# A hint for a taken branch, given later: in the middle of the small products in front of the branch

## The chip, the cores and the metric

The kernel runs on one core of one Trainium2 chip. The metric is the device time of one execution in microseconds. Times below are counted from the start of the profiled span. A core has five engines that run their own instruction streams: TensorE (PE; its sequencer, which also starts the weight loads, is shown as PEld or PEq), VectorE (DVE), ScalarE (ACT), GpSimd (POOL) and SyncE (SP), which here only issues DMAs and branches.

## The reference, cut to what matters

Three stages stand one behind the other: a local attention, a dense layer, and a layer of eight experts. Only the last one bears on the change:

```
do_compute = x @ w_skip > 0              # tokens that are computed at all
e_idx = argmax(x[do_compute] @ w_gate)   # the expert of each token
for e in range(8):
    rows = tokens of expert e
    h = maximum(x[rows] @ w1[e], 0)
    y[rows] = gate * (h @ w2[e])
out = x + y   (out = x for the tokens left out)
```

There are 1536 tokens of 512 numbers, and w1[e] is 512 x 1024. How many tokens an expert gets is known only at run time.

## The kernel before, in words

Attention and the dense layer take the first 440 us or so. Then a routing step sorts the tokens: each expert has one small tile of 32 tokens and, behind it, `nt[e]` full tiles of 128 tokens, a number that every engine loads into a register (`pre`, L711, a TENSOR_LOAD).

The function `experts()` (from L687 on) goes through the experts in turn, in an order written out by hand, so that each engine runs its instructions as the code lists them.

- **Full tiles.** They stand behind a branch, `tc.If(nt[e] > 0)` at L738. Inside it one tile is computed by `tile_e` (products at L589 and L606, transposes at L600), then `tc.If(nt[e] > 1)` at L746 and so on, up to a loop for a fourth tile and more. In the program the code of the full tiles stands right behind the branch; the branch is *taken* if there is no full tile, and then it jumps over all of that code.
- **Small tiles.** Behind the full tiles of expert e come the first small products of expert e + 1 (`mm1_s`, L659: 16 products in the program, 32 passes in the trace) and the second small products of expert e (`mm2_s`, L677: 32 in the program, 64 passes), a transpose for the next full tile (`tx`, L575), and a transpose of the small tile (`th_s`, L667). Then the next expert's branch follows. They read raw weights from a ring of 20 buffers, which SP fills (`load_e`, L542).
- **Hints.** `hint(e, n)` emits two instructions on TensorE alone: a comparison of `nt[e]` with n into a register, and a BRANCH_PREFETCH_HINT that reads it. With 0 in the register it says that the branch at level n of expert e will be taken; with 1, that it will not be. All instructions of a hint have L1116 in the trace. `hint(e, 0)`, for the outer branch, is given once for each expert; the inner ones are given at the head of each full tile.

Before, `hint(e + 1, 0)` stands right behind expert e's full tiles, ahead of all small products; for expert 0 it stands ahead of the transpose of the first small tiles (`tx_s`, L650).

Of the kernel before, what the change touches and what calls it, by code (L numbers as in the profile page):

```python
# [20 lines left out]
E, F = 8, 1024  # L21
# [40 lines left out]
def body(ctx: ExitStack, tc: tile.TileContext, a):  # L62
# [482 lines left out]
    def wraw(e, k):  # L545
        return raws[(8 * e + k) % NRAW]

    def split_e(e, k, c, sh=5):
        w, r = hl[k], wraw(e, k)
        A.activation(out=w[0][:, c], in_=r[:, c], func=AF.Copy)  # L550
        m = c.start + (c.stop - c.start) * sh // 8
        for eng, d in ((V, slice(c.start, m)), (G, slice(m, c.stop))):
            if d.start < d.stop:
              eng.tensor_tensor(out=w[1][:, d], in0=r[:, d], in1=w[0][:, d].bitcast(F32), op=ALU.subtract)  # L554
# [3 lines left out]
    def gather(xg, ix):  # L558
        nc.gpsimd.indirect_dma_start(out=xg, out_offset=None, in_=xs[:, :],
                                     in_offset=IndirectOffsetOnAxis(ap=ix, axis=0))  # L560

    def scatter(ix, xg):
        nc.gpsimd.indirect_dma_start(out=a["out"], out_offset=IndirectOffsetOnAxis(ap=ix, axis=0),  # L563
                                     in_=xg, in_offset=None, bounds_check=NT - 1, oob_is_err=False)
# [7 lines left out]
    def tx(xg, i):  # L572
        ps = psa.tile([128, 4, 128], F32, tag="a", name="pstx")
        for k in range(4):
            T.transpose(ps[:, k, :], xg[:, k * 128:(k + 1) * 128], ident)  # L575
        split_t((sl["x"][:, i, 0:4], sl["x"][:, i, 4:8]), ps)
# [66 lines left out]
    def ga_s(g):  # L643
        xsm[g] = gp.tile([128, DM], F32, tag="xg", name="xsm", bufs=2)
        gather(xsm[g], col(idx, E, g))

    def tx_s(g):
        ps = psa.tile([128, 4, 128], F32, tag="a", name="pstxs")
        for k in range(4):
            T.transpose(ps[:, k, :], xsm[g][:, k * 128:(k + 1) * 128], ident)  # L650
        for i in range(2):
            A.activation(out=xq[g][i], in_=ps[:, 2 * i:2 * i + 2], func=AF.Copy)

    def mm1_s(e):
        ps = psh.tile([128, 256], F32, tag="h", name="ps1")
        o = SM * (e % 4)
        for k in range(4):
            for j in range(4):
                T.matmul(out=ps[32 * j:32 * j + 32], lhsT=xq[e // 4][k // 2][:, k % 2, o:o + SM],  # L659
                         rhs=wraw(e, k)[:, 256 * j:256 * j + 256], start=(k == 0), stop=(k == 3))  # L660
        hsm[e] = sl["hr"]
        A.activation(out=hsm[e], in_=ps, func=AF.Relu)

    def th_s(e):
        ps = psa.tile([128, 2, 128], F32, tag="a", name="psths")
        for c in range(2):
            T.transpose(ps[:, c, :], hsm[e][:, c * 128:(c + 1) * 128], ident)  # L667
        hsm[e] = sl["hq"]
        A.activation(out=hsm[e], in_=ps, func=AF.Copy)

    def mm2_s(e):
        po = pso.tile([128, 128], F32, tag="o", name="pos")
        for f in range(8):
            w = wraw(e, 4 + f // 2)
            for j in range(4):
                o = 512 * (f % 2) + 128 * j
                T.matmul(out=po[32 * j:32 * j + 32], lhsT=hsm[e][:, f % 2, 32 * (f // 2):32 * (f // 2) + 32],  # L677
                         rhs=w[:, o:o + 128], start=(f == 0), stop=(f == 7))
        o, g = SM * (e % 4), e // 4
        for j in range(4):  # L680
            x = xsm[g][o:o + SM, 128 * j:128 * j + 128]
            V.scalar_tensor_tensor(out=x, in0=po[32 * j:32 * j + 32], scalar=col(gat, E, g)[o:o + SM], in1=x,  # L682
                                   op0=ALU.mult, op1=ALU.add)
        if e in SC:
            o = SC[e]
            n = SM * (e % 4 + 1)
            scatter(sl["ix"] if o else col(idx, E, g)[0:n], xsm[g][o:n])  # L687

    def col(t, e, j):
        return t[:, e * NJ + j:e * NJ + j + 1]  # L690

    def experts():
        sl["x"] = xts.tile([128, 2, 8, 128], F32R, tag="xt", name="slx")
        sl["h"] = xts.tile([128, 2, 8, 128], F32R, tag="xt", name="slh")
        sl["hr"] = ep.tile([128, 256], F32, tag="u", name="hr")
        sl["hq"] = ep.tile([128, 2, 128], F32, tag="n", name="hq")
        for g, tags in enumerate((("hn", "hn"), ("u", "n"))):
            xq[g] = [ep.tile([128, 2, 128], F32, tag=t, name=f"xq{g}{t}") for t in tags]
        xf = []
        for _ in range(2):  # L700
            t = stg.tile([128, 2, DM], F32, tag="stg", name="xh")
            xf.extend([t[:, 0], t[:, 1]])
        xf.extend(x2p.tile([128, DM], F32, tag="x2", name=f"xf{i}", bufs=3) for i in (4, 5))
        nt = {}

        def ga_f(e):
            if e < E:
                gather(xf[e % 3], col(idx, e, 1))

        def pre(e):  # L710
            nt[e] = nc.values_load(nti[0:1, e:e + 1], min_val=0, max_val=NJ - 1)  # L711

        def hint(e, n):
            tc.mark_branch_hint_location(f"t{n}{e}", hint=(nt[e] > n), engines=[mybir.EngineType.PE])

        def presplit(e):
            for k in range(4):
                split_e(e, k, C0, SH)

        sl["ix"] = rp.tile([SM, 1], I32, tag="r2", name="ix7")  # L720
        ga_s(0)
        ga_f(0)
        ga_f(1)
        ga_s(1)
        pre(0)
        hint(0, 0)
        presplit(0)
        tx_s(0)
        mm1_s(0)
        st["gates"]()  # L730
        tx(xf[0], 0)
        for e in range(E):
            fa, fb, fc, fd = xf[e % 3], xf[3], xf[4], xf[5]
            if e + 1 < E:
                pre(e + 1)
            if e < E - 1:
                th_s(e)
            with tc.If(nt[e] > 0, label=f"t0{e}"):  # L738
                hint(e, 1)
                gather(fb, col(idx, e, 2))  # L740
                tile_e(0, fa, col(idx, e, 1), col(gat, e, 1),
                       {0: [lambda k=k: split_e(e, k, C1, SI) for k in range(4)],
                        1: [lambda: split_e(e, 4, CA)], 2: [lambda: split_e(e, 5, CA)],
                        3: [lambda: split_e(e, 6, CA)], 4: [lambda: split_e(e, 7, CA)],
                        5: [lambda: tx(fb, 1)]})
                with tc.If(nt[e] > 1, label=f"t1{e}"):  # L746
                    hint(e, 2)
                    gather(fc, col(idx, e, 3))
                    tile_e(1, fb, col(idx, e, 2), col(gat, e, 2), {5: [lambda: tx(fc, 0)]})
                    with tc.If(nt[e] > 2, label=f"t2{e}"):  # L750
                        hint(e, 3)
                        tile_e(0, fc, col(idx, e, 3), col(gat, e, 3))
                        with tc.If(nt[e] > 3, label=f"t3{e}"):
                            with tc.For_i(3, nt[e], 1) as j:
                                ixd = rp.tile([128, 1], I32, tag="r1", name="ixd")
                                V.tensor_copy(ixd, idx[:, bass.ds(j + e * NJ + 1, 1)])
                                gtd = rp.tile([128, 1], F32, tag="r4", name="gtd")
                                V.tensor_copy(gtd, gat[:, bass.ds(j + e * NJ + 1, 1)])
                                gather(fd, ixd)
                                tx(fd, 1)  # L760
                                tile_e(1, fd, ixd, gtd)
            load_e(8 * e + 4 + NRAW)
            ga_f(e + 2)
            if e + 1 < E:
                hint(e + 1, 0)
                presplit(e + 1)
                mm1_s(e + 1)
            if e == 2:
                tx_s(1)
            if e < E - 1:  # L770
                mm2_s(e)
            if e == E - 2:
                V.tensor_copy(sl["ix"], col(idx, E, 1)[128 - SM:128])  # L773
                th_s(E - 1)
            if e + 1 < E:
                tx(xf[(e + 1) % 3], 0)
            if e == E - 2:
                mm2_s(E - 1)
            load_e(8 * e + 8 + NRAW)

    two = const.tile([128, 1], F32, name="two")
# [118 lines left out]
    half = {}  # L900
# [156 lines left out]
    with tc.manual_schedule():  # L1057
        experts()
# [61 lines left out]
```

## Time and profile before

| what | value |
| --- | --- |
| median of 3 runs | 605.8 us (605.23 to 607.18) |
| profiled execution | 607.17 us, its span 605.3 us |
| TensorE (PE) busy | 529.5 us, 87% of the span |
| VectorE, GpSimd, ScalarE busy | 451.4, 325.1, 293.5 us |
| first hint on TensorE | at 448.6 us |
| instruction queue q8 | 39 packets, 0.64 MB |

The span is cut into stages with different limits, so the shares say little; the last 157 us, from the first hint on, are those of the experts. The queues named "instruction" bring program code to the engines; they are listed with the other DMA queues. A row with PEldq or PEq is an instruction of TensorE's sequencer that does no arithmetic, such as a branch.

### The profile page before, as it was taken

What the parts mean: (1) busy time and instruction counts of PE and PEld (TensorE: products, weight loads), DVE (VectorE), ACT (ScalarE), POOL (GpSimd) and SP (SyncE); (2) the same over time, 40 slices, a digit from 0 to 9 for tenths busy, and PEclk for the clock granted to TensorE, in tenths of its full rate; (3) what the DMA queues carried; (4) which work ended last, traced back from release to release, by engine and by line L of the source; (5) the groups of instructions that cost most, each with busy time, mean ns of one, the idle gap of its engine ahead of it and who ended that gap; (6) DMA issues with size and microseconds to landing.
All of it is one profiled execution on the core that took longest, in us unless ns stands there. A gap on an engine that the chain in (4) does not pass through costs nothing. (4 is left out here: it accounts for less than half of the span.)

```text
span 605.3 us, 11155 instructions
## 1 busy us (share of the span) xinstructions
PE 529.5 (87%) x3870; PEld 429.3 (71%) x3870; DVE 451.4 (75%) x892; ACT 293.5 (48%) x614; POOL 325.1 (54%) x346
## 2 busy tenths in 40 slices
PE   6679768578887999999999999999879979698994
PEld 3557547457766888898988888988547857476873
DVE  3488999999999866659689697697677357466324
ACT  2746544446454646545444436444526346366321
POOL 5135767766667756435444445445547456667303
PEclk9889798899997999999999999999999999799998
DMA  8919543545421102224100037560137659991100
GB/s 272 322 42 316 158 162 129 173 152 142 125 64 32 47 21 76 86 70 157 34 15 15 1 139 247 206 208 2 58 107 272 228 178 390 324 370 48 35 18 15
DMA packets 40614, 82.57 MB, mean 136 GB/s; under 512 B 4749, under 2 KB 17297, under 8 KB 40536
## 3 DMA queue, kind: packets, MB, share of 16 engines
q1 hardware_dynamic: 38280, 75.03, 36.7%
q0 software_dynamic: 2256, 6.57, 3.4%
q8 instruction: 39, 0.64, 0.4%
q14 instruction: 39, 0.32, 0.2%
HBM read 72.92 MB, written 9.44 MB: 136 GB/s over the span
## 5 line engine op out<-in xcount | busy, mean ns | idle before, releaser
L373 PE MATMUL o<-w,g 128*128 128x512 f32 x576 | 158.0, 411 | 18.9 <-ACT g L343 17.2
L298 PE MATMUL h<-xt,w 128*128 128x384 f32 x768 | 158.6, 350 | 10.4 <-DVE hn L330 5.0
L298 PEld LDWEIGHTS h<-xt,w 128*128 128x128 f32 x768 | 137.5, 194 | 20.0 <-DVE hn L330 8.1
L373 PEld LDWEIGHTS o<-w,g 128*128 128x128 f32 x576 | 105.9, 192 | 44.9 <-ACT g L343 22.7
L331 POOL TENSOR_TENSOR hn<-hn,u 128x384 f32<-128x384 f32 (+1 forms) x66 | 81.1, 1229 | 67.3 <-ACT u L320 30.8
L344 POOL TENSOR_TENSOR g<-hn,g 128x384 fp32r<-128x384 f32 (+1 forms) x66 | 72.3, 1095 | 61.9 <-ACT g L343 61.8
L319 ACT ACTIVATE u<-nn,two 128x384 f32<-128x384 f32 (+1 forms) x66 | 40.0, 606 | 61.0 <-DVE nn L318 60.8
L187 POOL TENSOR_TENSOR w<-r,w 128x512 fp32r<-128x512 f32 x32 | 46.8, 1466 | 42.4 <-ACT w L186 42.4
L554 POOL TENSOR_TENSOR hl<-rawe,hl 128x128 fp32r<-128x128 f32 (+1 forms) x64 | 56.1, 904 | 14.6 <-ACT hl L550 14.0
L343 ACT ACTIVATE g<-hn 128x384 fp32r<-128x384 f32 (+1 forms) x66 | 33.8, 513 | 55.1 <-DVE hn L339 54.3
L339 DVE SCALAR_TENSOR_TENSOR hn<-nn,hn 128x384 f32<-128x384 f32 (+1 forms) x66 | 46.8, 709 | 15.3 <-POOL hn L331 15.1
L318 DVE SCALAR_TENSOR_TENSOR nn<-u 128x384 f32<-128x384 f32 (+1 forms) x66 | 48.0, 728 | 12.5 <-ACT u L312 12.4
L335 DVE SCALAR_TENSOR_TENSOR nn<-nn,u 128x384 f32<-128x384 f32 (+1 forms) x66 | 46.2, 699 | 13.8 <-ACT u L320 13.7
L554 DVE TENSOR_TENSOR hl<-rawe,hl 128x384 fp32r<-128x384 f32 (+1 forms) x64 | 43.6, 719 | 16.4 <-ACT hl L550 14.7
L550 ACT ACTIVATE hl<-rawe 128x512 fp32r<-128x512 f32 (+1 forms) x64 | 43.2, 731 | 11.9 <-PEq L738 4.3
L312 ACT ACTIVATE u<-u 128x384 f32<-128x384 f32 (+1 forms) x66 | 34.0, 515 | 30.8 <-DVE u L311 30.0
L589 PE MATMUL p<-hl,slx 128*128 128x512 f32 x168 | 41.8, 397 | 2.1 <-ACT slx L567 1.6
L606 PE MATMUL po<-hl,slh 128*128 128x512 f32 x168 | 43.1, 399 | 0.0
L311 DVE TENSOR_SCALAR u<-h 128x384 f32<-128x384 f32 (+1 forms) x66 | 35.5, 537 | 4.6 <-PE h L298 4.6
L589 PEld LDWEIGHTS p<-hl,slx 128*128 128x128 f32 x168 | 30.7, 188 | 9.1 <-ACT slx L567 2.3
L606 PEld LDWEIGHTS po<-hl,slh 128*128 128x128 f32 x168 | 30.6, 188 | 6.2
L320 ACT ACTIVATE u<-u 128x384 f32<-128x384 f32 (+1 forms) x66 | 33.6, 510 | 1.1
(175 smaller groups left out, 793.3 us busy)
## 6 DMA issues: line engine op xcount, KB each, us to landing
rawe<-w SPq DMA_DIRECT2D x64, 512.0 KB, 5.8
rawr<-wio SPq DMA_DIRECT2D x30, 512.0 KB, 3.8
vw<-vx SPq DMA_DIRECT2D x40, 97.5 KB, 2.9
xs<-x SPq DMA_DIRECT2D x12, 256.0 KB, 3.9
out<-x SPq DMA_DIRECT2D x12, 256.0 KB, 2.1
kw<-kx SPq DMA_DIRECT2D x18, 160.0 KB, 5.0
q<-qx SPq DMA_DIRECT2D x20, 128.0 KB, 3.4
kt<-kt SPq DMA_DIRECT2D x4, 384.0 KB, 4.2
```

Source lines behind the costliest of these rows:

```text
L187: G.tensor_tensor(out=w[1][:, o:o + 512], in0=r, in1=w[0][:, o:o + 512].bitcast(F32), op=ALU.subtract)
L298: T.matmul(out=h, lhsT=w[wi][:, k * 128:(k + 1) * 128], rhs=x[:, xi, k, :], start=(c == 0), stop=(c == 11))
L318: V.scalar_tensor_tensor(out=nn[:, c], in0=u[:, c], scalar=2.0, in1=u[:, c], op0=ALU.add, op1=ALU.mult)
L331: G.tensor_tensor(out=hn[:, c], in0=hn[:, c], in1=u[:, c], op=ALU.mult)
L335: V.scalar_tensor_tensor(out=nn[:, c], in0=nn[:, c], scalar=2.0, in1=u[:, c], op0=ALU.add, op1=ALU.mult)
L339: V.scalar_tensor_tensor(out=hn[:, c], in0=nn[:, c], scalar=2.0, in1=hn[:, c], op0=ALU.subtract, op1=ALU.mult)
L344: G.tensor_tensor(out=g[:, 1, c], in0=hn[:, c], in1=g[:, 0, c].bitcast(F32), op=ALU.subtract)
L373: T.matmul(out=o_t[t], lhsT=g[:, gi, t * 128:(t + 1) * 128], rhs=w[wi][:, 512:1024], start=(first and i == 0), stop=(end and i == 2))
L550: A.activation(out=w[0][:, c], in_=r[:, c], func=AF.Copy)
L554: eng.tensor_tensor(out=w[1][:, d], in0=r[:, d], in1=w[0][:, d].bitcast(F32), op=ALU.subtract)
L589: T.matmul(out=ps, lhsT=x[:, xi + k, :], rhs=w[wi][:, 512 * half:512 * half + 512], start=(k == 0 and xi == 0 and wi == 0), stop=(k == 3 a ...
L606: T.matmul(out=ps, lhsT=hs[f // 4][:, xi + f % 4, :], rhs=w[wi][:, 512 * (f % 2):512 * (f % 2) + 512], start=(f == 0 and i == 0), stop=(f ...
```

## The change

The hint for an outer branch is given later. For expert 0 it moves behind `mm1_s(0)`. For every other expert it moves into the middle of the last group of `mm2_s` ahead of its branch: `mm2_s` gets an argument, a function that it calls after 4 of its 8 steps. For experts 1 to 6 that group is `mm2_s(e)` of the expert before; for expert 7, whose branch has two such groups in front of it, it is `mm2_s(7)`, the later one.

```
-    def mm2_s(e):
+    def mm2_s(e, half=None):
         po = pso.tile([128, 128], F32, tag="o", name="pos")
         for f in range(8):
+            if f == 4 and half:
+                half()
             w = wraw(e, 4 + f // 2)
...
-        hint(0, 0)
         presplit(0)
         tx_s(0)
         mm1_s(0)
+        hint(0, 0)
...
             if e + 1 < E:
-                hint(e + 1, 0)
                 presplit(e + 1)
                 mm1_s(e + 1)
...
             if e < E - 1:
-                mm2_s(e)
+                mm2_s(e, None if e == E - 2 else lambda: hint(e + 1, 0))
...
             if e == E - 2:
-                mm2_s(E - 1)
+                mm2_s(E - 1, lambda: hint(E - 1, 0))
```

On TensorE's stream, ahead of expert 0's branch, it stood so before (pstxs: the small tiles' transpose, ps: `mm1_s`, psi: gates, pstx: `tx`, psths: `th_s`; lines of the kernel before):

```order
L714 REGISTER_ALU
L1116 BRANCH_PREFETCH_HINT
L650 MATMUL pstxs<-cb,xsm 128x128 x4
L659 MATMUL ps_4890<-rawe_3951,xq0hn 32x256 x4
L659 MATMUL ps_4890<-rawe_3953,xq0hn 32x256 x4
L659 MATMUL ps_4890<-rawe_3955,xq0hn 32x256 x4
L659 MATMUL ps_4890<-rawe_3957,xq0hn 32x256 x4
L495 MATMUL psi<-so 128x104 x6
L575 MATMUL pstx<-cb,xh 128x128 x4
L711 TENSOR_LOAD nti
L667 MATMUL psths<-cb,hr 128x128 x2
L738 COMPARE_AND_BRANCH
```

and so it stands now:

```order
L650 MATMUL pstxs<-cb,xsm 128x128 x4
L659 MATMUL ps_4887<-rawe_3951,xq0hn 32x256 x4
L659 MATMUL ps_4887<-rawe_3953,xq0hn 32x256 x4
L659 MATMUL ps_4887<-rawe_3955,xq0hn 32x256 x4
L659 MATMUL ps_4887<-rawe_3957,xq0hn 32x256 x4
L716 REGISTER_ALU
L1117 BRANCH_PREFETCH_HINT
L495 MATMUL psi<-so 128x104 x6
L575 MATMUL pstx<-cb,xh 128x128 x4
L713 TENSOR_LOAD nti
L667 MATMUL psths<-cb,hr 128x128 x2
L740 COMPARE_AND_BRANCH
```

The hint and its comparison have moved behind the five rows of transposes and `mm1_s`; 12 products, a register load and the waits in between are left ahead of the branch.

Ahead of expert 2's branch TensorE's stream was (pos: `mm2_s` of expert 1):

```order
L1116 BRANCH_PREFETCH_HINT
L659 MATMUL ps_5805<-rawe_4321,xq0hn 32x256 x4
L659 MATMUL ps_5805<-rawe_4323,xq0hn 32x256 x4
L659 MATMUL ps_5805<-rawe_4368,xq0hn 32x256 x4
L659 MATMUL ps_5805<-rawe_4370,xq0hn 32x256 x4
L677 MATMUL pos<-rawe_4199,hq 32x128 x8
L677 MATMUL pos<-rawe_4201,hq 32x128 x8
L677 MATMUL pos<-rawe_4250,hq 32x128 x8
L677 MATMUL pos<-rawe_4252,hq 32x128 x8
L575 MATMUL pstx<-cb,xh 128x128 x4
L711 TENSOR_LOAD nti
L667 MATMUL psths<-cb,hr 128x128 x2
```

and is now:

```order
L659 MATMUL ps_5802<-rawe_4323,xq0hn 32x256 x4
L659 MATMUL ps_5802<-rawe_4368,xq0hn 32x256 x4
L659 MATMUL ps_5802<-rawe_4370,xq0hn 32x256 x4
L679 MATMUL pos<-rawe_4199,hq 32x128 x8
L679 MATMUL pos<-rawe_4201,hq 32x128 x8
L716 REGISTER_ALU
L1117 BRANCH_PREFETCH_HINT
L679 MATMUL pos<-rawe_4250,hq 32x128 x8
L679 MATMUL pos<-rawe_4252,hq 32x128 x8
L575 MATMUL pstx<-cb,xh 128x128 x4
L713 TENSOR_LOAD nti
L667 MATMUL psths<-cb,hr 128x128 x2
```

The hint has moved behind all of `mm1_s` and half of `mm2_s`. The other engines' streams and the number of TensorE's instructions are as before.

## Rows read from the trace of the kernel before

**Rows 1.** The page's first line.

```profile
span 605.3 us, 11155 instructions
```

**Rows 2.** Line 738, TensorE's queue, experts 0, 2, 4, 7: ns min/median/max, start.

```profile
L738 PEldq COMPARE_BRANCH  x1: 1124/1124/1124, 455.0 to 455.0; - x1
...
L738 PEldq COMPARE_BRANCH  x1: 1494/1494/1494, 491.8 to 491.8; - x1
...
L738 PEldq COMPARE_BRANCH  x1: 5687/5687/5687, 518.9 to 518.9; - x1
...
L738 PEldq COMPARE_BRANCH  x1: 2792/2792/2792, 597.3 to 597.3; - x1
```

**Rows 3.** Line 1116, TensorE's hints ahead of the first three.

```profile
L1116 PEldq BRANCH_PREFETCH_HINT  x1: 44/44/44, 448.6 to 448.6; - x1
...
L1116 PEldq BRANCH_PREFETCH_HINT  x1: 39/39/39, 487.4 to 487.4; - x1
...
L1116 PEldq BRANCH_PREFETCH_HINT  x1: 35/35/35, 514.5 to 514.5; - x1
```

**Rows 4.** Windows: length; busy PE, PEld, DVE, ACT, POOL; clock, DMA share, GB/s.

```profile
197.80:419.10 221.30, 219.63 (x1397) 192.46 (x1394) 173.64 (x402) 109.79 (x219) 112.05 (x97) 1.00 0.28 90
455.00:457.00 2.00, 1.21 (x15) 0.89 (x18) 1.40 (x4) 0.96 (x3) 1.06 (x1) 1.00 0.05 14
...
459.00:460.00 1.00, 1.00 (x45) 1.00 (x39) 1.00 (x2) 0.37 (x2) 1.00 (x3) 1.00 0.89 184
...
487.40:490.00 2.60, 2.40 (x57) 1.96 (x61) 2.19 (x5) 2.17 (x5) 1.42 (x2) 1.00 0.18 65
...
518.90:522.10 3.20, 0.77 (x6) 0.53 (x6) 2.10 (x5) 0.87 (x2) 1.78 (x3) 1.00 0.94 262
```

**Rows 5.** Queue q8, windows 197.8:419.1, 453.5:454.8, 456.7:457.8, 490.9:491.9, 513.1:517.5.

```profile
q8 instruction: 11, 0.18, 0.4%
...
q8 instruction: 1, 0.02, 5.1%
...
q8 instruction: 1, 0.02, 5.4%
...
q8 instruction: 1, 0.02, 6.1%
...
q8 instruction: 1, 0.02, 1.6%
```

**Rows 6.** TensorE's timeline ahead of expert 3 and behind expert 4's branch.

```profile
499.54 0.42 PE L677 MATMUL pos<-rawe,hq 128*32 128x128 f32 x6 [1.37 <-issue]
...
525.05 1.94 PE L659 MATMUL ps<-rawe,xq1u 128*32 128x256 f32 x16 [5.38 <-PEq L738]
```

**Rows 7.** TensorE's timeline around expert 0's branch: start, us, group, idle before.

```profile
452.53 1.93 PE L659 MATMUL ps<-rawe,xq0hn 128*32 128x256 f32 x32 [0.53 <-ACT xq0hn L652]
454.39 0.87 PE L495 MATMUL psi<-so 128*128 128x104 f32 x6
...
456.75 1.93 PE L659 MATMUL ps<-rawe,xq0hn 128*32 128x256 f32 x32 [0.79 <-ACTq L738]
458.50 2.04 PE L677 MATMUL pos<-rawe,hq 128*32 128x128 f32 x64
...
461.86 4.40 PE L589 MATMUL p<-hl,slx 128*128 128x512 f32 x18 [0.52 <-issue]
```

**Rows 8.** Waits from 446 to 470 us: who waited for whom, us, times.

```profile
SPq L542 <- DVEq L738: 7.9, 1, 7.9
```

**Rows 9.** TensorE near 188 us; windows of TensorE: length, busy, clock, DMA share, GB/s.

```profile
187.77 2.10 PE L373 MATMUL o<-w,g 128*128 128x512 f32 x6 [2.98 <-ACT g L343]
...
188.80:195.60 6.80, 6.22 (x21) 0.50 0.00 1
...
525.00:530.10 5.10, 5.05 (x64) 0.50 1.03 396
```

**Rows 10.** The chain that ended last: start, us, what.

```profile
596.75 3.09 DMA out<-xsm,idx
```

More of the change, by code (lines that the diff above doesn't have):

```diff
@@ L669, in th_s, with mm2_s @@
         A.activation(out=hsm[e], in_=ps, func=AF.Copy)
-    def mm2_s(e):
+    def mm2_s(e, half=None):
         po = pso.tile([128, 128], F32, tag="o", name="pos")
         for f in range(8):
+            if f == 4 and half:
+                half()
             w = wraw(e, 4 + f // 2)
@@ L725, in experts @@
         pre(0)
-        hint(0, 0)
         presplit(0)
@@ L729, in experts @@
         mm1_s(0)
+        hint(0, 0)
         st["gates"]()
@@ L764, in experts @@
             if e + 1 < E:
-                hint(e + 1, 0)
                 presplit(e + 1)
@@ L770, in experts @@
             if e < E - 1:
-                mm2_s(e)
+                mm2_s(e, None if e == E - 2 else lambda: hint(e + 1, 0))
             if e == E - 2:
@@ L777, in experts @@
             if e == E - 2:
-                mm2_s(E - 1)
+                mm2_s(E - 1, lambda: hint(E - 1, 0))
             load_e(8 * e + 8 + NRAW)
```

## The prediction

> **What bounds the kernel now.** I read the page first and then, for the last quarter of the span, the timeline of TensorE, because that is where the hints stand. There the kernel is one chain on TensorE: eight experts in turn, each with small products on raw weights (L659, L677) and, if the expert has full tiles, the large products (L589, L606) behind a branch at L738. All the rows are from one execution of 607.17 us, whose span is 605.3 us [rows 1]; the median of three runs is 605.8 us. I work with differences and add them to the median.
>
> The branch of an expert without a full tile is taken. That is so for experts 0, 2, 4 and 7, and TensorE's sequencer sat in these four branches for 1.12, 1.49, 5.69 and 2.79 us [rows 2]. A branch that is not taken is quick, and I see nothing to win there. So the question is what sets these four numbers. The hints of the first three stand at 448.6, 487.4 and 514.5 us [rows 3], which is 6.4, 4.4 and 4.4 us ahead of their branches. The lead alone does not explain the wait: two equal leads have 1.5 and 5.7 us behind them.
>
> What explains it is the instruction queue. In a straight run of 221 us it brought 11 packets, 0.18 MB in all, while TensorE started 1397 products and 1394 weight loads [rows 4, 5]; that is one packet of 16 KB for each 254 or so instructions. Counting the built program in steps of 256 from a place where TensorE ran dry (1.37 us without a releaser, six passes before the end of an L677 group [rows 6]) gives the block edges:
> - One edge lies in the warming products just ahead of the first hint. No packet comes from there to 453.5, then one [rows 5]; the branch at 455.0 ends at 456.1. That packet was the branch's target.
> - Expert 2's hint at 487.4 has no packet behind it for 3.5 us, though the DMA was far from busy (0.18 [rows 4]). The packet comes at 490.9 [rows 5], as the sequencer passes an edge inside L677, and the branch ends at 493.3.
> - Expert 4's hint has no edge between it and its branch. The one packet of 513.1 to 517.5 [rows 5] belongs to the code behind the landing of expert 3. The target comes only once the branch asks: 5.69 us.
>
> [...] A hint decides what the next packet is, but the packet is asked for only when an edge is passed (or just has been); with no edge to come, the branch has to ask for itself.
>
> [...]
>
> **The change part by part.** Nothing is added or removed: a register operation and a hint (28 to 44 ns of queue time [rows 3]) move within each group, and the blocks keep their places.
>
> *Expert 0.* The hint moves behind the products of L659, which TensorE runs from 452.53 to 454.4 [rows 7]; the sequencer is somewhat ahead, so I put the hint at 453.3. The edge was passed before 448. [...] So the branch asks for itself. What that costs: the DMA is almost idle there, with a share of 0.05 from 455 to 457 [rows 4]. At its landing at 456.1 the sequencer's next packet followed within 0.7 us, after 456.7 [rows 5]; a packet takes about 1.0 us (5.1% of 16 engines over 1.3 us is 1.06 us [rows 5]), and the branch of expert 2 ended 1.4 us after its packet did. 0.7 + 1.0 + 1.4 = 3.1 us instead of 1.1: **+2.0 us**. Bounds: if the hint is served at once, 453.3 + 3.1 = 456.4, so +0.3; if the branch is as slow as expert 4's, 5.7 - 1.1 = +4.6. I take the idle value, since expert 4's branch stood in a DMA share of 0.94 [rows 4].
>
> *The block behind that landing.* From the landing to the next edge there are about 130 instructions: all of L659 and half of L677. Before, TensorE passed that edge near 459.2, 3.1 us after landing, without a wait, since the packet was asked for at 456.7 in an idle DMA. Now it is asked for at 458.1, after the weight loads of SP have begun (they wait for VectorE's branch [rows 8]) and the share is 0.89 [rows 4]. The nearest row for a landing in a busy DMA is expert 2's: landing at 493.3, TensorE goes on at 499.54 [rows 2, 6], 6.2 us. So 458.1 + 6.2 = 464.3 against 458.1 + 3.1 = 461.2: **+3.1 us**. Bounds: 0 if the packet still comes in time; 3.6 if it is asked for later still. I take 3.1, the only such row.
>
> [...]
>
> *The clock.* TensorE would stand from 456.0 to 458.7. [...] After expert 4's stall, 16 passes of L659 took 1.94 us, where 32 took 1.93 [rows 6, 7]: the lower of the two levels. If it falls here, most of the slow stretch lies where TensorE waits for the block anyway. **+0.6 us**, between 0 and 3.4 (half of 6.8).
>
> *Expert 2.* The new hint still stands some 29 instructions ahead of the edge inside L677, so the same packet is asked for at the same edge: **0**. Bounds: -1.4 if the branch needs no wait at all, +4.2 if it has to ask (5.7 - 1.5).
>
> *Expert 4.* No edge before, none now; the branch asks for itself either way: **0**. Bounds: nothing to lose; the most to win is the 5.6 us of the wait plus half of the 5 us at half speed behind it.
>
> *Expert 7.* Its branch is behind TensorE's last product. The chain ends in the scatter and its landing from 596.75 to 599.84 [rows 10], not in this branch; an edge lies between hint and branch both before and after: **0**, with some 4 us of room before the end of the span at 605.3.
>
> *Experts 1, 3, 5, 6.* Their hints say that the branch is not taken. They leave the place just behind a landing. **0**; bounds -1.4 (the wait at 499.54, if the hint delays that packet) and +3.6 (a packet dropped because expert 1's new hint stands right behind an edge).
>
> What passes through: ScalarE's and GpSimd's splits for expert 1 do not wait for the landing, and L589 at 461.86 already waits for TensorE's own chain alone [rows 7]; from there TensorE is busy without a gap. So the delay is carried to the end. Sum: 2.0 + 3.1 + 0.6 = 5.7 us, 612.9 us on the profiled execution, **611.5 us** on the median.
>
> **The rivals.**
> [...]
> - *A hint has a fixed delay.* If a hint asks at once but takes the time seen with experts 0 and 2 (7.5 and 5.9 us to the end of the branch), a shorter lead costs everywhere: +4.6 at expert 0 (capped by the branch's own asking), +2.3 at expert 2 (hint 2.3 us later), +3.1 for the block: 615.8 us. Against it: the packet of expert 2 came at an edge.
> - *Still in time.* The hint is served at once and quickly: 605.8 + 0.3 = 606.1 us. [...]
> - *Faster: expert 4's hint was lost and no longer is.* At 514.5 the packet behind the landing was still outstanding; a hint given then may be dropped. The new one comes near 516.9, once that packet (of 513.1 to 517.5) is under way. If it then is served with 3.1 us, the branch ends at 520.0 instead of 524.6: -4.6, and the half speed from 525.0 to 530.1 goes [rows 9], -2.5. It decides if it beats the +5.7 of expert 0: 605.8 + 5.7 - 7.1 = 604.4 us, and 602.9 with half of the block term. [...]
>
> **How the numbers follow.** Forecast 0.56, with its own range 608.0 to 615.5; only the branch pays 0.11; fixed delay 0.08; still in time 0.12; faster 0.13. About 0.3%, 1.8 us, is what a measurement of this kernel can tell from no change. Slower by more: 0.54 of the forecast, 0.07 of the second, all of the third: 0.69. Within: 0.02 + 0.04 + 0.12 = 0.18. Faster: 0.13. Leaving out about half of the faster case below, and half of the fixed delay with the forecast's upper tail above, the range is 604.0 to 616.5.
>
> **What would show it.** In the profile of the changed kernel the taken branch of expert 0 lasts about 3.1 us instead of 1.12, with a packet after 455.5; a gap without a releaser of 2 to 3 us stands inside the first L677 group; L589 of expert 1 starts near 467 instead of 461.9; expert 2's branch stays at 1.5, expert 4's at 5.7. I am wrong if expert 0's branch stays under 1.5 us (the hint is served without an edge), or if expert 4's falls below 3 us (the earlier hint was lost).

## The result, and the profile after

The changed kernel is slower: 612.73 us in the median of 7 runs (610.38 to 614.82) beside 607.18 us of the kernel before in the same session (7 runs, 605.23 to 612.1). The ratio is 1.0073 with a 95% interval of 1.0044 to 1.0103, so +4.4 us, between 2.7 and 6.3; the two medians lie 5.6 us apart. The forecast, 611.5 on 605.8, is a ratio of 1.0094: inside the interval.

The profiled execution took 610.38 us; its page begins so, beside [rows 1]:

```profile
span 608.6 us, 11155 instructions
```

The spans differ by only 3.3 us, because in this execution the first branch comes 2.2 us earlier than before. Of that lead 1.5 us are there 25 us into the span and 2.1 by 50 us, long before the first hint. Kernels whose streams are the same up to this branch differ as much (454.97 before, 453.86 and 452.32 in else_3 and else_all below), so I compare from the first branch on: 150.3 us from there to the end of the span before, 155.8 after, +5.5.

The four taken branches (TensorE's queue, line 740 now; ns, start) and the first three hints answer to [rows 2, 3]:

```profile
L740 PEldq COMPARE_BRANCH  x1: 3393/3393/3393, 452.8 to 452.8; - x1
...
L740 PEldq COMPARE_BRANCH  x1: 1623/1623/1623, 493.5 to 493.5; - x1
...
L740 PEldq COMPARE_BRANCH  x1: 6602/6602/6602, 520.3 to 520.3; - x1
...
L740 PEldq COMPARE_BRANCH  x1: 3465/3465/3465, 599.8 to 599.8; - x1
...
L1117 PEldq BRANCH_PREFETCH_HINT  x1: 44/44/44, 450.7 to 450.7; - x1
...
L1117 PEldq BRANCH_PREFETCH_HINT  x1: 35/35/35, 491.2 to 491.2; - x1
...
L1117 PEldq BRANCH_PREFETCH_HINT  x1: 35/35/35, 518.0 to 518.0; - x1
```

Expert 0's branch went from 1.12 to 3.39 us, with the hint 2.1 us ahead of it instead of 6.3. Expert 2's stayed. Expert 4's and expert 7's rose by 0.9 and 0.7 us.

The instruction queue in the windows 450.6 to 452.5, 452.6 to 454.6 and 458.6 to 459.8 us (packets, MB, share of 16 engines), beside [rows 5]:

```profile
q8 instruction: 1, 0.02, 3.3%
...
q8 instruction: 1, 0.02, 2.7%
...
q8 instruction: 1, 0.02, 5.0%
```

The first packet starts at 451.40, 0.75 us behind the hint, and does not serve the branch. The second starts at 453.70, 0.95 us behind the branch's start, and lasts 0.88; the branch ends 1.56 us later. The third is the block behind the landing.

TensorE's timeline there (start, us, group, idle before) answers to [rows 7]:

```profile
450.06 1.93 PE L659 MATMUL ps<-rawe,xq0hn 128*32 128x256 f32 x32 [0.53 <-issue]
...
453.11 0.38 PE L667 MATMUL psths<-cb,hr 128*128 128x128 f32 x2
456.46 3.49 PE L659 MATMUL ps<-rawe,xq0hn 128*32 128x256 f32 x32 [2.96 <-PEq L740]
459.76 1.06 PE L679 MATMUL pos<-rawe,hq 128*32 128x128 f32 x31
461.08 1.29 PE L679 MATMUL pos<-rawe,hq 128*32 128x128 f32 x33 [0.26 <-issue]
...
463.70 1.66 PE L589 MATMUL p<-hl,slx 128*128 128x512 f32 x6 [0.52 <-ACT slx L567]
```

And two windows of it (length, busy PE, clock, DMA share, GB/s), beside [rows 4, 9]:

```profile
456.30:459.70 3.40, 3.24 (x32) 0.50 0.94 278
...
455.00:457.00 2.00, 0.54 (x8) 0.81 0.82 147
```

The reader is to see three things between the branch and L589 of expert 1, which took 6.9 us before and 10.9 now. TensorE stands 2.96 us for the branch. Then the same 32 passes of L659 take 3.49 us instead of 1.93, at a granted clock of 0.50. And the block behind the landing costs one gap of 0.26 us. Worked out: 2.27 (3393 - 1124 ns) + 1.56 + 0.26 = 4.1 us, the difference of the two stretches. The other 1.4 us of the 5.5 are +0.9 in expert 4's branch, +0.9 in the last landing and -0.4 in between. The landing, beside [rows 10]:

```profile
599.16 3.97 DMA out<-xsm,idx
```

### The profile page after: what moved, and what is told of

It reads as the page before. It is cut to its first block, busy times and chain, and to the rows that moved or that the text cites. A ratio compares the mean times of both kernels' runs of the same rounds, so it can differ in the third digit from the quotient of the medians.

```text
span 608.6 us, 11155 instructions
## 1 busy us (share of the span) xinstructions
PE 528.9 (87%) x3870; PEld 428.0 (70%) x3870; DVE 450.5 (74%) x892; ACT 293.2 (48%) x614; POOL 324.8 (53%) x346
## 5 line engine op out<-in xcount | busy, mean ns | idle before, releaser
L373 PEld LDWEIGHTS o<-w,g 128*128 128x128 f32 x576 | 106.1, 193 | 44.9 <-ACT g L343 22.5
L589 PE MATMUL p<-hl,slx 128*128 128x512 f32 x168 | 41.7, 397 | 2.1 <-ACT slx L567 1.6
L589 PEld LDWEIGHTS p<-hl,slx 128*128 128x128 f32 x168 | 30.7, 188 | 9.0 <-ACT slx L567 2.3
```

The source lines that it names most:

```text
L373: T.matmul(out=o_t[t], lhsT=g[:, gi, t * 128:(t + 1) * 128], rhs=w[wi][:, 512:1024], start=(first and i == 0), stop=(end and i == 2))
L589: T.matmul(out=ps, lhsT=x[:, xi + k, :], rhs=w[wi][:, 512 * half:512 * half + 512], start=(k == 0 and xi == 0 and wi == 0), stop=(k == 3 a ...
```

## The experiments

Each time stands beside that of the kernel before from the same session; "to the end" is from expert 0's branch to the end of the span of the profiled execution (before: 150.3 us). With single runs I read only the profile, since runs of the kernel before spread from 604 to 612 us (one of 2789 us is left out).

**Which hint costs the time?** Three kernels, all made from the kernel before.

```
first_only:  -        hint(0, 0)            # ahead of tx_s(0)
             +        hint(0, 0)            # behind mm1_s(0); all other hints as before
rest_only:   the change without its first part: hint(0, 0) stays ahead of tx_s(0)
no_first:    -        hint(0, 0)            # nothing in its place
```

> Only expert 0's hint is given late (behind its L659 products); the other hints stand as before. Theory (a hint sets the next packet, which is asked for at a block edge; expert 0's late hint has no edge left): all of the loss is here. The branch of expert 0 lasts 3.1 to 3.6 us instead of 1.12, L659 behind it runs slowly if the clock falls; 605.8 + 4 = about 1.006 to 1.008 of before. Rival (a hint needs a fixed time, so that every shorter lead costs): about half of the loss, 1.003 to 1.004, since expert 2 and 4 keep their leads.

> Expert 0's hint as before, all others late (middle of L677). Theory: no change, 0.998 to 1.002; branch of expert 0 at 1.1, of expert 2 at 1.5 +- 0.3, of expert 4 at 5.7 or a little more. Rival (fixed time): expert 2's branch rises to 3.5 us or more, 1.004. Rival (expert 4's early hint was lost): its branch falls below 3 us, 0.99.

> Expert 0 gets no hint at all, the others as before. Theory: the late hint of expert 0 did nothing, so this is the same as the late hint: branch 3.1 to 3.6 us, 1.006 to 1.008 of before. Rival (the late hint did start the fetch, about 2 us ahead of the branch): without it the branch lasts 5 to 5.7 us and the time is 1.009 or more.

Measured: first_only 613.76 against 607.59 us, ratio 1.0082 [1.0048, 1.0116]; rest_only 608.31, 1.0009 [0.9977, 1.0041]; no_first 612.90, 1.0079 [1.0054, 1.0104]. Expert 0's branch in first_only and in no_first:

```profile
L738 PEldq COMPARE_BRANCH  x1: 3427/3427/3427, 455.4 to 455.4; - x1
```

```profile
L737 PEldq COMPARE_BRANCH  x1: 3365/3365/3365, 454.8 to 454.8; - x1
```

So, within these intervals, the whole loss is the first hint's, and where the change puts it, the hint is worth nothing that can be measured: without any hint the branch and the time are the same. In both kernels, as in the changed one, the packet starts 0.95 to 0.97 us behind the branch's start.

rest_only also moved expert 4's branch, from 5.7 to 3.3 us, and gained nothing:

```profile
L740 PEldq COMPARE_BRANCH  x1: 3268/3268/3268, 517.1 to 517.1; - x1
```

I come back to that with the last group.

**A block edge, or the lead?** My prediction let a hint work only if TensorE passes a block edge behind it, that is, goes over from one block of the program to the next (a block is what one packet of q8 brings: 254 products and weight loads in the straight run of [rows 4, 5], some 256 instructions with the 32 of TensorE's semaphores among them). Five kernels vary the edge and the lead (the time from a hint to its branch) apart.

```
edge_early: STEPS: z14 -> z34     # 20 more warming pairs at the start; the edge lies 37 instructions earlier
mid_hint:   hint(0, 0) between tx_s(0) and mm1_s(0): 3.5 us ahead of the branch
half_hint:  hint(0, 0) in the middle of mm1_s(0): 2.5 us ahead
edge_late:  the changed kernel, z14 -> z92: the edge lies between the late hint and its branch
mid_early:  edge_early and mid_hint together
```

> Hints as before, but 20 more warming pairs (40 instructions) run on TensorE near the start, so that every block edge falls some 37 instructions earlier in the later code: expert 0's early hint now stands 52 instructions behind an edge and none follows ahead of the branch. The lead of 6.4 us stays. Theory: the branch of expert 0 lasts 3.1 to 3.6 us as with the late hint; expert 2's edge comes 1 us earlier, so its branch falls to 0.4 to 0.8; the dry spell ahead of expert 3 grows from 1.4 to about 2.4 us. Rival (fixed time): branch of expert 0 stays at 1.1, of expert 2 at 1.5.

> Expert 0's hint stands between the transposes (L650) and the products of L659, so about 3.6 us ahead of its branch instead of 6.3 (early) or 2.1 (late); the rest as before. Reading 1 (the packet follows a hint by about 4.9 us, whatever else runs): the packet is not there in time, the branch asks for itself and lasts 3.4 us. Reading 2 (the packet was only held up by the four gathers that run from 447.5 to 452.5): it comes about 1.4 us ahead of the branch as with the early hint, and the branch lasts 1.1 us. Reading 3 (first theory, no edge left after the hint): 3.4 us.

> The kernel before with expert 0's hint alone moved, into the middle of the 16 products of L659 ahead of the branch: a lead of 2.6 to 2.9 us, between the 2.1 us that was worth nothing and the 3.5 us that was enough. If the hint works at once and a packet takes 1 us and its unpacking 1.5: the branch ends 2.5 us behind the hint, so it takes about 1.1 us at most, 151 to 152 us from there to the end. If a hint needs over 3 us, the branch takes 3.4 us as without a hint, 155 to 157 us to the end. A value between (1.5 to 3 us) would say that the branch waits for the rest of a fetch that the hint had begun.

> The changed kernel with 78 more warming pairs (products and their weight loads) at the start, where TensorE waits anyway, so that a block edge lies some 12 instructions behind expert 0's late hint and 16 ahead of its branch. First theory (a packet is asked for only at an edge): the target comes 1 us behind the edge, about at the branch, and the branch of expert 0 takes 1.0 to 1.6 us; the time from that branch to the end is about 151 us. Rival (a lead of 2.1 us is too short wherever the edge lies): the branch takes 3.3 to 3.5 us, 155 to 157 us to the end. If the plain next block is fetched at that edge first and holds the queue, the branch takes over 3.5 us.

> Two edits that each left expert 0's branch at 1.1 us, together: 20 more warming pairs at the start, so that the plain next block is in 5 us before the hint and no packet is outstanding when it comes, and expert 0's hint behind the transpose of the small tiles (a lead of 3.5 us). First theory (a hint turns a packet that is asked for and has not begun into the target; when none is outstanding it asks by itself, but later than 3.5 us): no packet of the queue ahead of the branch, one 1.0 us behind its start, the branch 3.3 to 3.9 us, 154 to 157 us from its start to the end. Rival (a lead of 3.5 us is enough as such; the packet only waits until the gathers are through the DMA): a packet 1.1 us behind GpSimd's last gather ahead of the branch and 1.4 us ahead of the branch, which takes 1.1 us, 150 to 152 us to the end.

Measured for all kernels, by the trace, one execution each (the packet is the one that the branch waited for; its start is counted from the branch's start):

| kernel | lead of the hint, us | packet, us | branch, ns | to the end, us |
| --- | --- | --- | --- | --- |
| before | 6.3 | -1.4 | 1124 | 150.3 |
| edge_early | 6.3 | -1.5 | 1116 | 149.5 |
| mid_early | 3.75 | -1.65 | 880 | 149.3 |
| mid_hint | 3.5 | -1.4 | 1097 | 152.3 |
| half_hint | 2.5 | +0.96 | 3897 | 155.4 |
| after | 2.1 | +0.95 | 3393 | 155.8 |
| edge_late | 2.1 | +1.5 | 3834 | 160.4 |
| no_first | none | +0.96 | 3365 | 155.8 |

The times of the single runs were 606.55 (edge_early), 609.70 (mid_hint), 610.31 (half_hint), 629.81 (edge_late: the 78 pairs hold up the start by some 13 to 15 us and disturb more than the edge: from expert 2's branch to expert 3's it takes 13.8 us, 8.1 in the changed kernel) and 607.20 (mid_early). mid_hint's 152.3 us come from later places: its branches of experts 2, 4 and 7 took 1.0, 0.7 and 1.0 us more than before. My miss shows best in edge_early. Branch and hint, and then the queues in the windows 442.7 to 444.2, 444.2 to 453.6 and 453.6 to 455.0:

```profile
L738 PEldq COMPARE_BRANCH  x1: 1116/1116/1116, 455.2 to 455.2; - x1
...
L1116 PEldq BRANCH_PREFETCH_HINT  x1: 44/44/44, 448.9 to 448.9; - x1
```

```profile
q8 instruction: 1, 0.02, 5.4%
...
q0 software_dynamic: 232, 0.78, 27.5%
q14 instruction: 2, 0.02, 0.8%
...
q0 software_dynamic: 74, 0.24, 50.9%
q8 instruction: 1, 0.02, 4.5%
```

The plain next block was in by 444.1, 4.7 us ahead of the hint, and no edge followed. By my reading nothing should have come, and the branch should have taken 3.4 us. The target came all the same, ahead of the branch. Of the rest of that expectation one half held: expert 2's branch fell to 449 ns, but the dry spell ahead of expert 3, which was to grow, is gone. The reverse is edge_late: hint at 465.5, branch at 467.6, the edge (as the program is laid out) between them. Its queues from 445.4 to 469.0 and from 469.0 to 470.0:

```profile
L740 PEldq COMPARE_BRANCH  x1: 3834/3834/3834, 467.6 to 467.6; - x1
...
L1117 PEldq BRANCH_PREFETCH_HINT  x1: 35/35/35, 465.5 to 465.5; - x1
```

```profile
q0 software_dynamic: 560, 1.84, 22.9%
q1 hardware_dynamic: 432, 0.79, 9.2%
q14 instruction: 2, 0.02, 0.3%
...
q8 instruction: 1, 0.02, 5.7%
```

In the long window there is no row of q8 at all: neither edge nor hint brought a packet in time. So at expert 0 an edge behind the hint is not what it takes: hints 3.5 us and more ahead of the branch worked without one, and hints 2.1 us ahead did not work, with an edge or without, nor did one 2.5 us ahead.

Between the two I tried a last escape, that a hint can only turn a packet that is still outstanding, and asks too slowly by itself. mid_early refutes it; its branch and hint, and its queues from 444.8 to 454.3 and from 454.3 to 455.5:

```profile
L738 PEldq COMPARE_BRANCH  x1: 880/880/880, 456.1 to 456.1; - x1
...
L1116 PEldq BRANCH_PREFETCH_HINT  x1: 40/40/40, 452.3 to 452.3; - x1
```

```profile
q0 software_dynamic: 233, 0.78, 25.9%
q14 instruction: 2, 0.02, 0.7%
...
q0 software_dynamic: 58, 0.19, 54.8%
q8 instruction: 1, 0.02, 5.1%
```

Nothing was outstanding when the hint came, and its packet started 2.1 us later.

That the short lead itself is the cause is not shown. half_hint's branch and hint, and q8 from 449.8 to 451.2:

```profile
L739 PEldq COMPARE_BRANCH  x1: 3897/3897/3897, 453.0 to 453.0; - x1
...
L1117 PEldq BRANCH_PREFETCH_HINT  x1: 44/44/44, 450.4 to 450.4; - x1
...
q8 instruction: 1, 0.02, 4.7%
```

That packet, the plain next block's, ran from 449.91 to 450.97, across the hint. In the changed kernel and in first_only it started 0.75 and 0.5 us behind the hint; in edge_early, mid_hint and mid_early no such packet is near. So a late hint and a plain packet beside it mostly come together, and a rival stands: such a packet holds the hint's own back. Only edge_late has the short lead alone (the packet before its hint started at 444.4), and it is one disturbed execution. else_3 below bears on this too: its stream up to expert 0 is that of the kernel before and its hint stands 6.3 us ahead, but a plain packet came first, 2.1 us behind the hint, the target's 3.4 us after that one, and the branch took 1634 ns. No kernel was made that tells the lead from the packet.

**What holds the packet back?** In the kernel before it came 4.9 us behind the hint, in mid_hint and mid_early 2.1 us. Two kernels change what lies between.

```
late_gathers: ga_f(1), ga_s(1) moved from ahead of hint(0, 0) to behind presplit(0)
fill_behind:  FW = (4, 4, 4, 16) -> (4, 4, 4, 4), and behind hint(0, 0) the same 12 warming products
```

> Hints as before, but the third and fourth gather on GpSimd (experts 1's tile and the second group of small tiles) are issued behind the splits of expert 0, so that less DMA runs between expert 0's hint and its branch. Reading 1 (fixed 4.9 us): packet 4.9 us behind the hint, branch 1.1 us. Reading 2 (held up by the gathers): packet 2 to 3.5 us behind the hint, branch under 0.3 us, and TensorE goes on about 0.9 us earlier against the branch's start.

> Hints as before, but 12 of the 16 warming products in front of expert 0's register load run behind its hint, so that the hint stands 9 instructions ahead of a block edge instead of 15 behind it; the hint still cannot run before the register is loaded (at 448). First theory (the packet is asked for at an edge): packet about 1 us behind the hint, the branch of expert 0 under 0.3 us, 0.998 of before. Reading 1 or 2 (4.9 us, or the gathers): packet 4 to 5 us behind the hint, branch 1.1 us, 1.000.

late_gathers: one run of 611.09 us against 608.57; the packet starts 3.8 us behind the hint and 2.6 us ahead of the branch, which takes 479 ns. fill_behind: 607.33 against 608.57, ratio 0.9993 [0.9969, 1.0017]; the packet starts 5.3 us behind the hint and 2.35 us ahead of the branch, 479 ns again. With half of the gathers moved back by some 1.6 us the packet came 1.1 us sooner behind the hint. In the kernel before, edge_early, mid_hint and mid_early it starts 0.8 to 1.1 us behind the end of GpSimd's fourth gather, in fill_behind 1.5. Both fit a packet that waits behind the gathers in the DMA; they do not prove it, since in late_gathers it comes 2.6 us behind the end of the second gather and while the third is being issued. What is shown is that the branch of the kernel before could still be 0.65 us shorter, and that this alone is too little to be seen in the time.

**Expert 4's branch.** Its stall of 5.7 us was the prize of my "faster" rival. Two kernels give its hint earlier, in the arm that runs when expert 3 has no further tile.

```
else_3:    with c1.Else(): hint(e + 1, 0)     # for e == 3 alone, in place of the hint behind the tiles
else_all:  the same in the Else of every level c0 to c3, for every expert
```

> The hint for expert 4's branch stands in the else arm of expert 3's second condition, that is at the landing of the branch before it, some 1.3 us earlier than before; for this run's data that path is taken. All else as before. If a hint given within a microsecond of a landing takes the place of the next plain packet, expert 4's branch falls from 5.7 us to under 2.5 and the slow clock behind it goes with it: 0.988 to 0.993 of before. If the packet follows the hint by 4.9 us or more in a busy DMA, counted from the landing at 513.1: packet at 518 to 519.5 instead of 522.1, the branch lasts 1.5 to 3.5 us: 0.990 to 0.996. If the hint is lost behind the landing's own packet: branch 5.7 us, 1.000.

> The kernel before, but the hint for the next expert's outer branch is given where it is known that no further tile follows: in the else arm of every level of the full tiles. With this data that moves it into the jump's landing of expert 3 and alike; the hint of expert 0 stays early. Theory (the lead up to the branch counts, and the packet needs room): expert 4's branch falls from 5.7 to under 3 us as when expert 3's first level alone had it, expert 2's stays at 1.5 to 2.7 us, and the time is 0.993 to 0.998 of before, most of the 3 us at the branch being given back behind it, where the weights' DMAs set the pace. Rival (the some nine further hints for each expert shift the block edges and the gain at expert 3 was such a shift): expert 4's branch stays at 5 to 7 us and the time is 1.000 of before, between 0.998 and 1.004.

else_3: 605.46 against 608.57 us, ratio 0.9958 [0.9936, 0.9981]. else_all: 604.25 against 607.25, ratio 0.9948 [0.9929, 0.9967]. Both beat the kernel before, and so the changed one, and neither does so for my reason. Expert 4's branch in else_3, and its timeline and clock 25 us later:

```profile
L738 PEldq COMPARE_BRANCH  x1: 2072/2072/2072, 517.9 to 517.9; - x1
```

```profile
543.48 0.65 PE L659 MATMUL ps<-rawe,xq1u 128*32 128x256 f32 x3 [3.60 <-issue]
```

```profile
542.00:549.00 7.00, 5.53 (x81) 0.54 0.51 169
```

The same place in rest_only, and in the kernel before:

```profile
544.43 0.41 PE L659 MATMUL ps<-rawe,xq1u 128*32 128x256 f32 x2 [2.80 <-issue]
```

```profile
547.42 0.41 PE L659 MATMUL ps<-rawe,xq1u 128*32 128x256 f32 x3 [0.50 <-issue]
```

From expert 4's branch to expert 5's, else_3 takes 6.1 us instead of 12.2; from there to expert 6's it takes 24.7 instead of 19.5. What the branch gave is lost again behind expert 5's tile: 3.60 us without a releaser (0.50 before), while a packet of the queue is on its way, and then half of the clock. Why that packet comes so late there is not shown. rest_only does the same with -3.1 and +3.3. In the profiled executions the sum to the end is 150.6 us in else_3 and 150.0 in else_all, against 150.3.

else_all does not even shorten that branch, though its hint stands 6.4 us ahead, where else_3's stands 5.0:

```profile
L742 PEldq COMPARE_BRANCH  x1: 7343/7343/7343, 517.4 to 517.4; - x1
```

What it does win stands ahead of expert 7's, behind expert 6's tiles. There the kernel before has a gap that else_all has not, and this is part of it; the two timelines:

```profile
592.61 0.41 PE L659 MATMUL ps<-rawe,xq1n 128*32 128x256 f32 x3 [0.94 <-issue]
```

```profile
588.70 1.07 PE L659 MATMUL ps<-rawe,xq1u 128*32 128x256 f32 x16 [0.58 <-PEq L757]
589.56 1.07 PE L659 MATMUL ps<-rawe,xq1n 128*32 128x256 f32 x16
590.42 1.96 PE L677 MATMUL pos<-rawe,hq 128*32 128x128 f32 x64
```

From expert 6's branch to expert 7's it takes 44.5 us instead of 46.8, as edge_early (44.9) and mid_early (44.8) do, whose edges are shifted too; +1.9 at expert 4 and smaller terms take most of it back. So the rival of that expectation is right about expert 4 and wrong about the time. Why the many runs gain 2.6 and 3.2 us by their ratios where the profiled executions, from the first branch on, gain -0.3 and 0.3, is open.

## Why the prediction was right, and where it was not

*The branch of expert 0.* Right in place and size: 3.39 us for the 3.1 predicted. The three parts were 0.7, 1.0 and 1.4; they measured 0.95 (branch to packet), 0.88 (packet) and 1.56 (packet to landing).

*Why it has to ask for itself.* This step failed: "the packet is asked for only when an edge is passed (or just has been)". edge_early and mid_early got the target by a hint with no edge behind it, and edge_late did not get it with one. edge_early fetched the plain next block at 442.8 and the target at 453.7 while the block in work went on; no run shows whether the first was dropped. What the runs put in its place is a pattern at expert 0: hints 2.1 and 2.5 us ahead were worth nothing, hints 3.5 us and more ahead worked. Whether the lead does it or the plain packet beside the late hints stays open. I forecast the right branch for a wrong reason, and the reason would have misled anyone who used it to place a hint: mid_hint, which it condemns if the edge lies elsewhere, works. The lead is no law either. else_all's hint for expert 4, 6.4 us ahead, left a branch of 7.3 us in a busy DMA (0.97 from 517.4 to 522.3 us). Expert 2's late hint had 2.3 us, and its packet came within 1.2 us of it, in the changed kernel and in rest_only; there an edge does follow, and edge_early, whose edge is earlier, has that branch at 449 ns. No plain packet ran in the 3 us ahead of these two hints, so the rival above would explain it as well as the edge does. Why 2.5 us fail in one place and 2.3 serve in another is not settled.

*The block behind the landing.* Mis-sized: 3.1 us predicted, 0.26 measured (0.19 in no_first, 1.24 in half_hint, 1.71 in first_only). I took the only row of a landing in a busy DMA, 6.2 us until TensorE goes on, against 3.1 us of work up to the edge. Here TensorE went on 4.9 us behind the landing (456.14 to 461.08), and at the lower clock the work up to the edge took 1.56 us longer, which hid most of the wait. At full clock the gap would have been some 1.8 us, an estimate from these two numbers. The gap of 2 to 3 us that I named as a sign did not come.

*The clock.* Mis-sized the other way: 0.6 predicted, 1.56 measured. The bound's 6.8 us is the first stretch at 0.50 in [rows 9]; here the clock was 0.50 for 3.4 us. I let the slow stretch fall on the wait for the block; it was the other way round, the slow stretch covered the wait. The two errors, -2.8 and +1.0, partly cancel.

*Experts 2, 1, 3, 5, 6.* Nothing, as predicted. *Expert 7*: its branch went from 2.8 to 3.5 us, and stands beside the last landing, as said.

*Expert 4.* The branch kept asking for itself, 6.60 us instead of 5.69; with the same hint rest_only has 3.27. I had no term for such a spread; rest_only's ratio of 1.0009 shows no gain from the shorter branch.

*The rivals.* "Only the branch pays" (605.8 + 2.0 = 607.8 us) missed the clock. "Fixed delay" falls with mid_hint: 2.1 us from hint to packet, not 4.9. "Still in time" falls with no_first: the late hint is worth no more than none. "Faster" fell, and its price was wrong by more than its mechanism: of the 7.1 us I gave for expert 4's stall nothing is left in the profiled executions of rest_only and else_3, and 2.6 us at most by the ratios, while TensorE runs dry for longer behind expert 5's tile.

*The sum.* 5.7 predicted, 4.1 at expert 0 in the trace, 4.4 by the ratio. That the profiled executions differ by 5.5, so near to it, is luck: 1.4 of it lies at expert 4 and in the last landing, which I had put at 0, and at expert 0 two errors cancel in part.

## What to carry to other kernels

Test a hint against no hint before its place is tuned: if the branch takes as long as with none, it is worth nothing where it stands, as 2.1 to 2.5 us ahead of expert 0's branch, where 3.5 us was enough. Do not carry these leads to another branch: experts 2 and 4 do not follow them. A shorter stall at one branch can be lost again behind a later one, as in rest_only and else_3; add up the segments between the branches, not the branches. And count the slow clock behind a stall as a term of its own: here stalls of 2.96 and 3.60 us had granted clocks of 0.50 and 0.54 behind them.

## What was not expected of the hardware

- A hint given 2.1 us ahead of expert 0's taken branch changed nothing measurable: 3393 and 3427 ns with it, 3365 ns without one.
- A taken branch whose target is not there took 3.4 to 3.9 us at expert 0 (DMA share 0.07 from 452.75 to 455.0 in the changed kernel) and 5.7 to 7.3 us at expert 4 (share 0.94 from 518.9 to 522.1 [rows 4]).
- Twenty more warming pairs at the start of the program took 1 us off expert 2's branch (1494 to 449 ns) and 2 us off the way from expert 6's branch to expert 7's, in edge_early and again in mid_early. The stream behind the pairs is the same, so the shifted block edges are the likely cause; nothing else was varied to prove it.
- Extra work at the start was not always free: 20 pairs were, 78 pairs were not (first branch at 467.6 instead of 455.0 us).
